# Loading the first two chunks of a gated recurrence as one pair, and re-planning the order of all engines, in a fused attention and gated MLP kernel

## The chip, the core and the metric

The kernel runs on one core of a Trainium2 chip. The core has five engines, each with its own queue of instructions that runs strictly in the order in which the program issued them: TensorE (PE, matrix products), VectorE (DVE), ScalarE (ACT), GpSimd (POOL) and SyncE (SP), which here only issues transfers. Sixteen DMA engines move data between the main memory and the on-chip memory. The metric is the device time of one execution in microseconds; the span of a profile is a little shorter, since it begins with the first instruction.

## What is computed

The first half is a gated recurrence over 768 steps for 4 batches and 8 heads with a state of 48 x 48; the second half is a gated MLP whose gate mixes the time steps with a matrix.

```python
# first half: q, k, v, alpha are (4, 8, 768, 48), float32
for t in range(S):
    state = alpha[:, :, t, :, None] * state + einsum('bhd,bhe->bhde', k[:, :, t], v[:, :, t])
    y[:, :, t] = einsum('bhd,bhde->bhe', q[:, :, t], state)

# second half: x is y as (4, 768, 384); d_ff = 1024
h = maximum(x @ w_in, 0)
u, v = h[..., :512], h[..., 512:]
v_n = (v - mean(v)) / sqrt(var(v) + 1e-6)
v_s = einsum('ts,bsd->btd', w_spatial, v_n) + b_spatial[None, :, None]
out = (u * v_s) @ w_out                      # (4, 768, 384), float32
```

## The kernel before

The 768 steps of a batch are cut into 6 chunks of 128, so there are 24 chunks, numbered through all four batches. A chunk turns the recurrence into matrix products: the logarithm of alpha (Ln on ACT), its running sum by a product with a triangle of ones (`cum`), two exponentials, the scaled keys and queries (`kt`, `qt`), their transposes, the scores, a causal mask, and the output `y`; beside it a state of 48 x 48 per head is carried from chunk to chunk (`upd`, `z`, `S`, `sb`).

There are two forms of this work. `first(i)` treats one chunk: each of its four loads brings 128 x 8 runs of 48 floats. `pair(j)` treats two neighbouring chunks at once: time steps 2p and 2p+1 lie side by side on partition p, so each load brings 128 x 8 runs of 96 floats for both chunks, and the running sum, scores and `y` are split into an even and an odd half (`par`) with two triangles (`le_pair`, `lt_pair`) and another mask (`mask2`).

```python
PAIRS = (1, 2)                     # chunks 2,3 and 4,5 go as pairs; all others one by one

def first(i):                      # one chunk
    def load(name, src):
        ...
        nc.sync.dma_start(out=t, in_=src[b, :, t0:t0 + C, :].rearrange("h s d -> s h d"))
    dma(("ac", i), LD, load("ac", alpha), ...)     # then kc, qc, vc
    ...

def pair(j):                       # chunks 2j and 2j+1
    def load(name, src):
        ...
        nc.sync.dma_start(
            out=t.rearrange("p h a d -> p h (a d)"),
            in_=src[b, :, t0:t0 + 2 * C, :].rearrange("h (p a) d -> p h (a d)", a=2))
    ...                            # ac, kc, qc, vc
    op(("lnp", j), "ACT", 0.73, ln, got(("ac", 2 * j), ("cz", 2), ("cz", 0)) + ...)
    for par in range(2):
        # cump, einvp, eexpp, ebc, ktp, qtp, vbp, transposes tr, evictions ev
        op(("ktp", j, par), {"POOL": 0.87, "DVE": 0.47}, ...)
        ...
```

The program's order is found before it is built. Every piece of work is an `Op` with a duration for each engine that may do it, and `schedule` places them one by one on the engine where they can start earliest; a table of small delays or advances (`PATIENCE`) bends the choice. What it decides is the order in each engine's queue, and which engine does an operation. Wherever the plan leaves TensorE idle in the first 40 us (`WARM`), it puts in products of a tile `junk` that nobody reads, which keep TensorE's clock up.

```python
def dma(key, us, emit, deps, prio, eng="SP", issue=0.99, lat=1.9):
    o = op(key + ("issue",), eng, issue, emit, deps, prio=prio)
    return op(key, "DMA", us, lambda _: None, [o], prio=prio, lat=lat)

o.wait = PATIENCE.get(key[0], 0.0)
```

The constants come first in the queues of DVE (memsets) and POOL (triangles and masks). Those of single chunks come ahead, those of pairs after them:

```python
def constants(_):
    nc.gpsimd.memset(ut_ones, 0.0)          # triangle of single chunks
    nc.vector.memset(junk, 0.5)
    nc.vector.memset(lap_bufs[0].bitcast(FP32), 0.0)
    ... # select on ut_ones, ident
    nc.vector.memset(mask4.bitcast(FP32), 0.0)
    nc.gpsimd.affine_select(out=mask4, ...) # mask of single chunks

def zeros(n):
    # n == 0: second set of la, kt, qt;  n == 1: sbd, ones_row, eps, lt_pair, mask2 to zero
    # n == 2: le_pair, lt_pair and the four quarters of mask2, by selects on POOL
    ...
```

The second half works in groups on one bank of the accumulation memory: `v` (x with the second half of w_in, then the mean and variance of each row, `bn`), `u` (first half of w_in), `s` (the mix over time, then the bias and the product with u), `o` (w_out). The output tiles are copied by ACT and stored; the last four go into the space that the raw weights have left, and the very last is copied by ACT and DVE, one half each. All of that is in the kernel before and stays.

Of the kernel before, what the change touches and what calls it, by code (L numbers as in the profile page):

```python
# [9 lines left out]
FP32 = mybir.dt.float32  # L10
BF16 = mybir.dt.bfloat16
AF = mybir.ActivationFunctionType
ALU = mybir.AluOpType
# [38 lines left out]
class Clock:  # L52
# [21 lines left out]

PATIENCE = {"ev": -0.3, "v": -0.1, "be": 0.2, "g": -0.3, "sb": -0.1, "bb": 0.5, "ln": 0.2, "z": -0.2, "we": -0.1, "S": 0.3, "cast": -0.1, "rs": 0.1, "trk": -0.1, "xs": -0.3}
ENGINES = {
    "kt": {"POOL": 0.87},
    "vb": {"POOL": 0.47},
    "S": {"POOL": 0.57},
    "sb": {"POOL": 0.79, "DVE": 0.36},  # L80
# [5 lines left out]
}  # L86
PAIRS = (1, 2)
ACT_STATS = ((2, 2), (1, 4), (1, 2))
PIECES = {
    "w_in": ((0, "vc", 0, 0.35), (0, "kc", 2, 0.15)),  # L90
    "w_sp": ((0, "vc", 4, 0.35), (0, "ac", 7, 0.05), (0, "ac", 7, 0.05)),
    "w_out": (0, "kc", 7, 0.15),
# [48 lines left out]
def kernel(  # L141
# [12 lines left out]
    nc = tc.nc  # L154
# [37 lines left out]
    fill = []  # L192
# [45 lines left out]
    def constants(_):  # L238

        nc.gpsimd.memset(ut_ones, 0.0)  # L240
        nc.vector.memset(junk, 0.5)  # L241
        nc.vector.memset(lap_bufs[0].bitcast(FP32), 0.0)
        nc.vector.memset(ones_col, 1.0)
        nc.gpsimd.affine_select(
            out=ut_ones, in_=ut_ones, compare_op=ALU.is_gt, fill=1.0,
            base=0, channel_multiplier=1, pattern=[[-1, 128]],
        )
        for t in (ktp_bufs[0], qtp_bufs[0]):
            nc.vector.memset(t.bitcast(FP32), 0.0)
        make_identity(nc, ident)  # L250
        nc.vector.memset(mask4.bitcast(FP32), 0.0)
        nc.gpsimd.affine_select(
            out=mask4, in_=mask4, compare_op=ALU.is_gt, fill=1.0,
            base=0, channel_multiplier=1, pattern=[[0, 4], [-1, 128]],
        )

    def zeros(n):

        def emit(_):
            if n == 0:  # L260
                for t in (lap_bufs[1], ktp_bufs[1], qtp_bufs[1]):
                    nc.vector.memset(t.bitcast(FP32), 0.0)
            if n == 1:
                for t in sbd_bufs:
                    nc.vector.memset(t.bitcast(FP32), 0.0)
                nc.vector.memset(ones_row, 1.0)
                nc.vector.memset(eps_tile, LN_EPS)
                nc.vector.memset(lt_pair.bitcast(FP32), 0.0)
                nc.vector.memset(mask2.bitcast(FP32), 0.0)
            if n == 2:  # L270
                nc.gpsimd.memset(le_pair, 0.0)
                for t, base in ((le_pair, 0), (lt_pair, 1)):
                    nc.gpsimd.affine_select(
                        out=t, in_=t, compare_op=ALU.is_gt, fill=1.0, base=base, channel_multiplier=1,
                        pattern=[[-1, 128]],
                    )
                    nc.gpsimd.memset(t[0:64, 64:128], 0.0)
                for par in range(2):
                    for ci in range(2):
                        rows = slice(64 * ci, 64 * ci + 64)  # L280
                        nc.gpsimd.affine_select(
                            out=mask2[rows, par], in_=mask2[rows, par], compare_op=ALU.is_gt, fill=1.0,
                            base=par, channel_multiplier=2, pattern=[[0, 4], [-1, 2], [-2, 64]],
                        )
        return emit
# [4 lines left out]
    def op(key, *args, **kw):  # L290

        users = kw.pop("use", ())
        o = Op(*args, **kw)
        for s in users:
            s.users.append(o)
        ops.append(o)
        made[key] = o
        o.wait = PATIENCE.get(key[0], 0.0)
        return o

    def got(*keys):
        return [made.get(x) for x in keys if x is not None]

# [85 lines left out]
    def pair(j):  # L389
# [30 lines left out]

        op(("lnp", j), "ACT", 0.73, ln, got(("ac", 2 * j), ("cz", 2), ("cz", 0)) + io_users("cum", jo, 0), prio=P + 1)
        sl_c = [Slot(rings["p2"]), Slot(rings["p2"])]
# [166 lines left out]
    def first(i):  # L589
# [15 lines left out]
        jo = j - NKP  # L605
        dma(("ac", i), LD, load("ac", alpha), io_users("ln", j), P)
        dma(("kc", i), LD, load("kc", k), io_users("kt", j), P + 0.1)
        dma(("qc", i), LD, load("qc", q), io_users("qt", j), P + 0.2)
        dma(("vc", i), LD, load("vc", v), io_users("vb", j), P + 0.3)

# [4 lines left out]

        op(("ln", i), "ACT", 0.41, ln, got(("ac", i), ("cz", 0) if j % NKP else None) + io_users("cum", jo, 0), prio=P + 1)

# [364 lines left out]
    op(("cz", 0), "DVE", 1.7, zeros(0), prio=-5.0)  # L982
    op(("cz", 1), "DVE", 1.3, zeros(1), prio=-4.0)
    op(("cz", 2), "POOL", 2.6, zeros(2), got(("cz", 1)), prio=-3.0)

# [38 lines left out]
    dma(("b_sp",), 0.1, lambda _: nc.gpsimd.dma_start(out=b_sp_sb, in_=moe_b_spatial[None, :]), [], 0.9, "POOL", 1.0)  # L1024
    late.append((made[("b_sp", "issue")], ("qc", 0)))
    for i in range(N):
# [56 lines left out]
```

## Time and profile before

The time is 159.15 us, the median of three runs (159.13 to 162.23). The profiled run has a span of 157.4 us with a granted clock of 1.0.

| What | Value |
|---|---|
| PE busy | 146.9 us, 93% of the span, 1719 matmuls |
| of it on `junk` | 15.1 us |
| DVE busy | 127.3 us, 81% |
| ACT busy | 108.4 us, 69% |
| POOL busy | 84.3 us, 54% |
| transfers | 28.6 MB, 97,173 packets, of which 92,032 under 512 B |
| first load issued, first Ln starts | 0.75 us, 3.77 us |
| last load issued | 108.85 us |
| last matmul ends | 153.7 us |

Read it as two questions. First, which engine is full in which stretch of the span, and how much of it is real work. Second, how early the first real work of each kind begins, since all later work of a full engine moves with it. A busy PE is not a PE at its peak: `junk` counts as busy.

### The profile page before, as it was taken

Reading aid. Unit: us, or ns where it says so; the run is one execution under the profiler, and the core shown is the slowest. Engines: PE = TensorE matmul, PEld = TensorE weight load, DVE = VectorE, ACT = ScalarE, POOL = GpSimd, SP = SyncE. Lnnn points to the kernel's source line nnn. Section 1 sums busy time; section 2 is a strip of 40 time slices with the busy share of each in tenths; the row PEclk is TensorE's granted clock in tenths of the full one; section 3 lists DMA queues with packets and bytes.
Section 4 is the critical chain, followed back from the end, with each engine's and each line's share of the span. In section 5 each row is a group of like instructions: output and inputs, shape, how many; then the busy total and the mean of one; then the engine's idle time right before and its main releaser. Section 6 shows DMA issues by size and latency. Waiting matters only on the chain.

```text
span 157.4 us, 4483 instructions
## 1 busy us (share of the span) xinstructions
PE 146.9 (93%) x1719; PEld 97.1 (62%) x1719; DVE 127.3 (81%) x271; ACT 108.4 (69%) x269; POOL 84.3 (54%) x141
## 2 busy tenths in 40 slices
PE   6849999998999998899999999999999999999990
PEld 5838577766667565456565657565675766556550
DVE  7617778879899999977899989899989989555820
ACT  3352786898897776589998465989996465891051
POOL 4684383645348754882236989654356956102420
PEclk9999999999999999999999999999999999999999
DMA  5999999989997999999897999998990000520034
GB/s 103 198 280 259 311 270 239 298 156 307 171 274 147 209 255 176 218 208 200 159 205 149 210 209 182 199 198 168 315 369 15 6 0 0 199 105 0 0 127 175
DMA packets 97173, 28.60 MB, mean 182 GB/s; under 512 B 92032, under 2 KB 95616, under 8 KB 97152
## 3 DMA queue, kind: packets, MB, share of 16 engines
q1 hardware_dynamic: 97120, 28.32, 77.6%
q8 instruction: 13, 0.21, 0.6%
q14 instruction: 8, 0.07, 0.1%
q0 software_dynamic: 32, 0.00, 0.0%
HBM read 23.60 MB, written 4.72 MB: 180 GB/s over the span
## 4 chain that ended last, share of the span: by engine, by line
PE 64%; DVE 22%; ACT 5%; issue 3%; POOL 3%; POOLq 0%; DVEq 0%
PE ps L774 38%; PE pt L671 4%; DVE ptm L712 4%; PE pt L701 3%; DVE vsb L914 2%; PE y L362 2%; DVE qt L654 2%; PE y L729 2%; DVE stats L836 2%; DVE sbd L209 2%; PE ps L199 2%; PE tp L687 2%; ACT x_sb L207 2%; DVE kqT L209 1%; PE y L723 1%
## 5 line engine op out<-in xcount | busy, mean ns | idle before, releaser
L927 POOL TENSOR_TENSOR gT<-vsb,uT 128x384 bf16<-128x384 f32 x28 | 25.5, 918 | 22.0 <-DVE vsb L914 21.6
L774 PE MATMUL ps<-w_spT,vn 128*128 128x384 bf16 x192 | 36.2, 326 | 0.3 <-DVE w_spT L209 0.3
L712 DVE TENSOR_TENSOR ptm<-pt,mask 128x512 bf16<-128x512 f32 x40 | 26.1, 682 | 2.0 <-PE pt L701 1.8
L644 POOL TENSOR_TENSOR kt<-kc,binv 128x384 bf16<-128x384 f32 x20 | 18.2, 914 | 13.3 <-ACT bc L639 9.0
L774 PEld LDWEIGHTS <-vn 128*128 128x128 bf16 x192 | 17.0, 97 | 10.8 <-issue 0.7
L333 POOL TENSOR_TENSOR state<-state,bc 128x192 f32<-128x192 f32 x20 | 10.3, 515 | 21.1 <-DVE state L328 14.0
L914 DVE TENSOR_TENSOR vsb<-ps,bsp_bc 128x384 f32<-128x384 f32 x31 | 16.6, 550 | 4.0 <-PE ps L774 3.5
L774 PE MATMUL ps<-w_in,xT 128*128 128x512 bf16 x72 | 19.4, 380 | 0.3
L207 ACT CAST x_sb<-y 128x384 bf16<-128x384 f32 x24 | 11.4, 477 | 10.4 <-PE y L729 8.9
L774 PE MATMUL ps<-xT,w_in 128*128 128x384 bf16 x96 | 18.4, 325 | 0.0
L774 PE MATMUL ps<-w_out_sb,gT 128*128 128x384 bf16 x96 | 18.1, 326 | 0.0
L209 DVE COPY kqT<-pt 128x1024 bf16<-128x1024 bf16 x17 | 11.5, 683 | 6.0 <-PE pt L671 5.9
L836 DVE BATCH_NORM_STATS2 stats<-v_sb 128x6 f32<-128x512 bf16 x18 | 12.3, 685 | 3.4 <-ACT v_sb L213 3.4
L213 ACT ACTIVATE v_sb<-ps 128x512 bf16<-128x512 f32 x18 | 10.8, 598 | 5.0 <-PE ps L774 4.6
L207 ACT COPY xT<-y 128x384 bf16<-128x384 bf16 x24 | 11.4, 480 | 3.5 <-PE y L362 3.2
L199 PEld LDWEIGHTS <-junk 128*128 128x128 bf16 x128 | 12.0, 109 | 2.3 <-DVE junk L241 1.1
L614 ACT ACTIVATE la<-ac 128x384 bf16<-128x384 f32 x20 | 10.4, 528 | 4.0 <-DMA ac<-in_alpha_dram 4.0
L209 POOL CAST vb<-vc 128x384 bf16<-128x384 f32 x20 | 10.1, 509 | 3.9 <-PE y L729 2.5
L774 PEld LDWEIGHTS <-gT 128*128 128x128 bf16 x96 | 8.8, 97 | 5.6
L866 DVE TENSOR_SCALAR vn<-v_sb,mvs,rstd 128x512 bf16<-128x512 bf16 x24 | 11.7, 521 | 0.2
L654 DVE TENSOR_TENSOR qt<-qc,cum 128x384 bf16<-128x384 f32 x20 | 10.8, 548 | 0.8 <-ACT cum L649 0.6
L774 PEld LDWEIGHTS <-w_in 128*128 128x128 bf16 x96 | 8.4, 97 | 4.6
(127 smaller groups left out, 299.2 us busy)
## 6 DMA issues: line engine op xcount, KB each, us to landing
ac<-in_alpha_dram SPq DMA_DIRECT2D x20, 192.0 KB, 4.1
kc<-in_k_dram SPq DMA_DIRECT2D x20, 192.0 KB, 4.1
qc<-in_q_dram SPq DMA_DIRECT2D x20, 192.0 KB, 4.1
vc<-in_v_dram SPq DMA_DIRECT2D x20, 192.0 KB, 4.1
raw_w<-in_moe_w_spatial_dram SPq DMA_DIRECT2D x3, 768.0 KB, 5.9
out_dram<-raw_w SPq DMA_DIRECT2D x12, 192.0 KB, 2.7
out_dram<-o_sb SPq DMA_DIRECT2D x9, 192.0 KB, 1.9
raw_w<-in_moe_w_in_dram SPq DMA_DIRECT2D x2, 768.0 KB, 6.5
```

The costliest lines, as they stand in the source:

```text
L199: nc.tensor.matmul(out=flat[:, 0:cols], lhsT=junk[:, 0:128], rhs=junk[:, 0:cols], start=True, stop=True)
L207: nc.scalar.copy(out=out, in_=in_)
L209: ENG[eng].tensor_copy(out=out, in_=in_)
L213: nc.scalar.activation(out=out, in_=in_, func=AF.Relu)
L644: ENG[eng].tensor_mul(out=kt[:, :, :, 0:D], in0=quad(st["kc"]), in1=st["binv"])
L654: nc.vector.tensor_mul(out=qt[:, :, :, 0:D], in0=quad(st["qc"]), in1=st["cv"])
L712: nc.vector.tensor_tensor(out=st["ptm"][:, s], in0=st[f"pt{s}"], in1=mask4, op=ALU.mult)
L774: return lambda ps: nc.tensor.matmul(out=out(ps), lhsT=lhsT(), rhs=rhs(), start=start, stop=stop)
L836: nc.vector.bn_stats(out=stats, in_=d["v_sb"][:, tt, :])
L866: nc.vector.tensor_scalar(out=d["vn"][:, t, :], in0=d["v_sb"][:, t, :], scalar1=d["mvs"][:, t, 0:1], scalar2=d["rstd"][:, t:t + 1], op0=AL ...
L914: nc.vector.tensor_tensor(out=hold["vs"], in0=ps[:, 0:TH], in1=bsp_bc[:, th, :], op=ALU.add)
L927: ENG[eng].tensor_tensor(out=bt[b]["gT"][:, dsl, cols], in0=hold["vs"], in1=bt[b]["uT"][:, dsl, cols], op=ALU.mult)
```

## The change

Chunks 0 and 1 are loaded and treated as a pair too, so that all six chunks of the first batch go as three pairs (`PAIRS = (0, 1, 2)`). It is for fewer and longer packets at the start and for two chunks in one pass. The constants of pairs now come ahead of those of single chunks, and the running sum of a pair no longer waits for the constants of single chunks.

The order is planned anew. The landing of a single chunk's load is planned at 2.9 us after its transfer time and no longer at 1.9 (`LATE`), while pairs and weights keep 1.9: hence uneven landings. A second table, `NUDGE`, delays or advances thirty named operations. `vb` may now go to ACT as well as POOL, the state's scaling `S` to DVE as well as POOL. One pair of `v` tiles whose statistics ACT computes is moved from batch 1 to batch 3, the last two pieces of the mixing matrix are loaded about one chunk earlier, and the load of the bias is issued after the first vc and no longer after the first qc.

The diff, with the cuts marked:

```diff
-PATIENCE = {"ev": -0.3, "v": -0.1, "be": 0.2, "g": -0.3, "sb": -0.1, "bb": 0.5, "ln": 0.2, "z": -0.2, "we": -0.1, "S": 0.3, ...}
+PATIENCE = {"ev": -0.3, "kt": -0.1, "v": -0.1, "sb": 0.3, "bb": 0.5, "ln": 0.2, "z": -0.2, "we": -0.1, "S": 0.2, ..., "xe": -0.2}
 ENGINES = {
-    "vb": {"POOL": 0.47},
-    "S": {"POOL": 0.57},
+    "vb": {"POOL": 0.47, "ACT": 0.42},
+    "S": {"POOL": 0.57, "DVE": 0.27},
 ...
-PAIRS = (1, 2)
-ACT_STATS = ((2, 2), (1, 4), (1, 2))
+NUDGE = {
+    ("o", 3, 0, "mm", 0): -0.15,
+    ("bn", 0, 1): -0.6,
+    ("kt", 6): 1,
+    ("ktp", 0, 0): -1.5,
+    ("v", 0, 4): -1.5,
+    ... # 25 more
+}
+PAIRS = (0, 1, 2)
+LATE = 2.9
+ACT_STATS = ((2, 2), (1, 4), (3, 4))
 PIECES = {
     "w_in": ((0, "vc", 0, 0.35), (0, "kc", 2, 0.15)),
-    "w_sp": ((0, "vc", 4, 0.35), (0, "ac", 7, 0.05), (0, "ac", 7, 0.05)),
+    "w_sp": ((0, "vc", 4, 0.35), (0, "qc", 6, 0.25), (0, "qc", 6, 0.25)),
 ...
     def constants(_):
-        nc.gpsimd.memset(ut_ones, 0.0)
         nc.vector.memset(junk, 0.5)
+        nc.gpsimd.memset(le_pair, 0.0)
+        nc.vector.memset(mask2[:, 0].bitcast(FP32), 0.0)
 ...     # selects for le_pair, lt_pair and mask2 move here from zeros(2);
 ...     # those for ut_ones and mask4 move to zeros(2)
-        o.wait = PATIENCE.get(key[0], 0.0)
+        o.wait = PATIENCE.get(key[0], 0.0) + NUDGE.get(key, 0.0)
 ...
-        op(("lnp", j), "ACT", 0.73, ln, got(("ac", 2 * j), ("cz", 2), ("cz", 0)) + ...)
+        op(("lnp", j), "ACT", 0.73, ln, got(("ac", 2 * j), ("cz", j - 1)) + ...)
 ...
-        dma(("ac", i), LD, load("ac", alpha), io_users("ln", j), P)
+        dma(("ac", i), LD, load("ac", alpha), io_users("ln", j), P, lat=LATE)
 ...     # the same for kc, qc, vc
-    late.append((made[("b_sp", "issue")], ("qc", 0)))
+    late.append((made[("b_sp", "issue")], ("vc", 0)))
```

The number of instructions in the queues changes as follows: four loads of 384 KB take the place of eight of 192 KB; PE has 117 products of `junk` in place of 128 and 58 products of other kinds more; DVE has 2 instructions more; ACT and POOL have as many as before, of other kinds.

## The prediction

> **What bounds the kernel now.** I read the busy shares and the slices first. The columns of the first five lines are busy time, share of the span and instructions; a digit below is the busy share of a slice of 3.9 us, in tenths.
>
> ```profile
> PE 146.9 (93%) x1719; PEld 97.1 (62%) x1719; DVE 127.3 (81%) x271; ACT 108.4 (69%) x269; POOL 84.3 (54%) x141
> ...
> PE   6849999998999998899999999999999999999990
> ...
> DVE  7617778879899999977899989899989989555820
> ACT  3352786898897776589998465989996465891051
> POOL 4684383645348754882236989654356956102420
> ...
> DMA  5999999989997999999897999998990000520034
> ```
>
> PE is at nine tenths from the fourth slice on, DVE nearly so from slice 8 to 33, the transfers from the second slice to the 31st. All three look like the bound, so I next asked for busy time by stretches (columns: stretch, length, then busy time and instructions of PE, PEld, DVE, ACT and POOL, granted clock, share of the DMA engines, GB/s).
>
> ```profile
> 8.00:12.00 4.00, 1.89 (x32) 1.42 (x32) 0.85 (x2) 2.17 (x5) 3.31 (x6) 1.00 1.07 276
> ...
> 36.00:40.00 4.00, 3.36 (x83) 2.79 (x81) 3.92 (x9) 2.96 (x8) 2.23 (x4) 1.00 1.07 293
> ...
> 116.00:128.00 12.00, 12.00 (x163) 8.27 (x160) 10.59 (x24) 7.72 (x19) 7.72 (x11) 1.00 0.19 67
> ```
>
> The same stretches for the line that issues `junk` alone give 15.11 us in all, of which 14.90 before 40 us and 0.21 after. So in the first 40 us PE is busy 35.3 us but does real work for only 20.4; after 40 us it is real work, 111.4 us in the 113.7 us up to the last matmul at 153.7. **The second part is a full PE with DVE just behind; only the first 40 us have room.** The transfers are no bound later: the last load is issued at 108.85 us, and 41 us of full PE follow its landing (some 4 us on). What does the start wait for? The timeline (start, duration, engine, line, operation):
>
> ```profile
> 0.75 0.43 SPq L601 DMA_DIRECT2D ac<-in_alpha_dram  x1
> ...
> 3.77 0.52 ACT L614 ACTIVATE la<-ac 128x384 bf16<-128x384 f32 x1 [1.74 <-DMA ac<-in_alpha_dram]
> ...
> 6.04 2.79 POOL L281 TENSOR_SCALAR_AFFINE_SELECT mask<-mask 64x512 bf16<-64x512 bf16 x4
> ...
> 9.53 0.91 POOL L644 TENSOR_TENSOR kt<-kc,binv 128x384 bf16<-128x384 f32 x1
> ...
> 17.38 0.81 PE L774 MATMUL ps<-w_in,xT 128*128 128x512 bf16 x3
> ...
> 21.41 0.81 PE L774 MATMUL ps<-w_in,xT 128*128 128x512 bf16 x3
> ```
>
> The first Ln is ready at 3.77 and its exponential `binv` at 5.44 (4.95 + 0.49), but the first `kt` starts at 9.53: POOL is still making the masks of pairs and issuing the bias's load. Four microseconds are lost there to constants that chunk 0 doesn't need. The last two lines are the `v` groups of chunks 0 and 1, four microseconds apart.
>
> **What the Trainium skill says.** "DMA: Bandwidth & Descriptors", section "Why small descriptors are slow (HBM only)", says that each packet has a fixed overhead, so short runs lose. The trace agrees: in 72 to 84 us, with single chunks alone, the engines move 190 GB/s at a share of 0.97; in 17 to 21 us, mostly pairs, 322 GB/s at 1.08. "TensorE: Matmul & The Clock Gate", section "What's actually happening", says that the array's clock is throttled until it has been active; the first 16 products of `junk` take 2.69 us here (168 ns each), 12 of them after 12.2 us take 1.15 (96 ns), so the filler is needed and its time is no saving by itself. "GPSIMD Engine Reference", section "Elementwise — side-by-side cycle accounting", puts an elementwise product of two tensors at 1.96 times DVE's time; here `kt` takes 912 ns on POOL and 552 on DVE, 1.65 times. This matters since the first `kt` half of the new pair goes to DVE.
>
> **The change, part by part.**
>
> *1. Transfers.* Eight loads of 196,608 B become four of 393,216 B with as many packets each (1024), so 4096 packets go. One single load is 196,608 / (190/0.97 GB/s) = 1.00 us of all 16 engines, one pair load 393,216 / (322/1.08) = 1.32 us. Saved: 4 x (2.00 - 1.32) = 2.7 us, all in the first ten microseconds of the stream. Every later load can land up to 2.7 us earlier; the order of bytes up to the second pair's vc is nearly the old one.
>
> *2. The first alpha.* It is twice as large: I add 0.3 us (1.32 - 1.00) to 3.77, so Ln starts at 4.1 and takes 0.84 for a pair, not 0.53.
>
> *3. The first pair's chain*, with durations of the second pair's rows: sums on PE 1.0 (two products with triangles of 0.33 and eight small ones of 0.04), to 5.95; `binv` 0.49, to 6.45. DVE's memsets add up to 5.2 us from 0.86, so it is free at 6.1 and does the first `kt` half to 7.0; POOL, with 5.3 us of selects, is free at about 6.8 and does the second (0.91) from 7.5 to 8.4. Queries: 8.8. Transposes and evictions (0.40 and 0.42 to 0.58): 9.9. vc lands at about 9 (2.9 us of latency as for the first load, four times 1.32, and the issue at 0.75) and its two casts on ACT share the time to 10.4. Scores to 10.9, four masks of 0.68 to 13.7, `y` of both chunks to 14.6, the cast, transpose and copy (0.48 + 0.34 + 0.48) to 15.9 and 16.3. So `v` of chunks 0 and 1 run at about 16.0 and 16.8 in place of 17.4 and 21.4: **1.4 and 4.6 us earlier.** The second half of w_in comes after five pair loads, as many bytes as before, and is cast by then.
>
> *4. The second pair.* Its `y` starts at 27.72 before. Its alpha comes fifth in the queue and its Ln can start at about 11 to 12, not at 17.20; its vc is 2.7 us earlier. DVE's queue up to its last mask holds about 21 us from 0.86 with the rows' means. I take `y` at 23 to 25: **3 to 5 us earlier.**
>
> *5. PE's own work.* By shape, a pair whose first chunk reads no state costs 1.1 (sums) + 0.67 (small) + 0.85 (scores) + 1.15 (`y`) + 0.35 (state) + 0.87 (`upd`) = 5.0 us; two single chunks 2 x (0.33 + 0.25 + 0.40 + 0.39 + 0.31) + 0.34 = 3.7. So 1.3 us more of real PE work, but at a time when PE has 15 us of filler; 11 fewer products of `junk` (about 1.1 us) take its place. Cost at the end: 0.
>
> *6. Moved work.* On DVE: eight casts of `sbd` fewer (-3.2), `kqT` +0.6, three `S` +1.05, two `uT` +1.1, one `gT` +0.6, one `kt` +0.55, weight casts -0.2: +0.5 us in 127, no relief. ACT gets five `vb` (+2.5) and gives up two `uT` (-1.0) and two weight casts: within 1 us. Nothing is taken off the engines that are full later.
>
> *Sum.* The front gains 3 to 5 us. Behind it the engines are full of unchanged work, and loads land early enough: chunk 6's alpha is issued at 23.27 and used at 33.17, chunk 8's at 35.73 and used at 47.04, so with 4.1 us to land 5 us or more are spare, and the loads come 2.7 us earlier themselves. So nearly all of the front's gain could reach the end. I take off about 1 us because the new order after 40 us can't be expected to leave PE less than the 2.3 us of idle that it has there now, and may leave more: expected -2.8 us, 156.4.
>
> **The rivals.**
> - *The old start isn't the bound.* If DVE decides in 22 to 60 us (it is busy 3.92 of 4 us in the line above for 36 to 40), an earlier `v` only fills queues behind it. For it: DVE's total grows by 0.5. Against it: DVE is idle for 3.15 us of 8 to 12 and itself waits for the start. It would make 158 to 159.5.
> - *The queue heads stop.* The plan keeps 1.9 us for a pair's landing, while pair loads take 6.1 us from issue to landing in the median and single ones 4.1. ACT's queue has the casts of vc ahead of the second pair's Ln, and PE has `y` ahead of the second pair's transposes. If vc lands 2 us later than I think, all of that waits, and the front gains 1 to 2 us only: 157.5 to 158.5.
> - *The new order is worse later.* Thirty nudges and other engines for `vb` and `S` re-arrange 110 us that are already 98% full on PE; 3 us of new idle would swallow the gain, 5 would turn it: 160 to 161.
> - *The stream of loads was the pace.* Then the time falls by the 2.7 us of transfers: 156.5, the same number by another way. What speaks against it is the 41 us after the last landing.
>
> **Range and chances.** The sum is 156.4. The low end takes the whole 5 us and a tidier middle; the high end the third rival in a mild form: 153.4 to 160.6. The 2% limits are at 156.0 and 162.3. My middle lies just above the first, so faster by over 2% gets 0.40, within 2% 0.47, slower 0.13.
>
> **What would show it.** Right: the first `kt` before 7.5 us, `v` of chunk 1 before 17.5, the second pair's `y` before 25.5, 93,000 packets, the last load issued 2 to 4 us earlier, and the last `junk` ahead of 37 us of real time. The step of the sum fails if these hold and the time doesn't fall: then PE's idle after 40 us has grown. The steps of the front fail if Ln of the first pair starts after 5 us, or if ACT's first cast of vc waits for its load for over a microsecond.

## The result, and the profile after

The changed kernel takes 157.48 us (median; 157.30 to 157.88) against 159.13 us for an undisturbed run of the kernel before: 1.6 us less. The ratio of all compared runs is 0.9899, with a 95% interval of 0.9867 to 0.9931. The forecast was 2.8 us less; the sign is right and the size is not. One sentence is needed to read the ratios: the kernel before runs at 159.1, 160.7 or 162.1 us with a mean TensorE clock of 1.00, 0.989 or 0.979, and ratios count the first two levels, so I also set each median beside 159.13.

The page of the changed kernel, the lines that answer to those of before (busy time, share, instructions; slices in tenths; the load queue's packets, MB and share of the 16 engines):

```profile
PE 145.3 (93%) x1766; PEld 95.7 (62%) x1766; DVE 127.6 (82%) x273; ACT 108.1 (69%) x269; POOL 83.2 (53%) x141
...
PE   7799799999999999897989998999999999999990
...
DVE  7777578598899899976999999889989999367830
...
q1 hardware_dynamic: 92960, 28.32, 77.9%
```

PE's third slice is 9 where it was 4, so the front is fuller. But slice 19 (70 to 74 us) has fallen to 7, and before no slice between the third and the last was below 8. The fifth (16 to 19 us) has fallen from 9 to 7 as well; more on it below. The busy time by stretches says it more exactly. Columns: stretch, length, busy time and instructions of PE, PEld, DVE, ACT and POOL, granted clock, share of the DMA engines, GB/s. Two stretches of the kernel before, then three of the changed one:

```profile
0.00:40.00 40.00, 35.30 (x535) 27.30 (x535) 29.55 (x68) 25.35 (x58) 22.79 (x49) 1.00 1.01 241
...
60.00:84.00 24.00, 22.63 (x247) 13.65 (x246) 21.18 (x46) 20.00 (x57) 11.51 (x19) 1.00 1.01 198
```

```profile
0.00:40.00 40.00, 36.52 (x597) 27.75 (x598) 30.08 (x71) 27.09 (x61) 22.82 (x49) 1.00 1.02 246
...
60.00:84.00 24.00, 21.61 (x252) 13.16 (x250) 21.17 (x45) 19.72 (x52) 12.68 (x22) 1.00 0.97 191
84.00:116.00 32.00, 31.32 (x388) 20.37 (x386) 29.93 (x62) 25.92 (x70) 19.50 (x32) 1.00 0.95 214
```

In 60 to 84 us PE is idle for 24.00 - 21.61 = 2.4 us (before: 24.00 - 22.63 = 1.4); the waits of that stretch name `qt` on DVE (0.7), `xT` and `uT` on ACT (0.8 and 0.7). With the line of `junk` taken out (13.21 us, all before 40), the end of the last matmul is a sum that can be compared ("real work" is PE's busy time less that of `junk`):

| PE, in us | before | after | difference |
|---|---|---|---|
| `junk` | 15.1 | 13.2 | -1.9 |
| real work up to 40 us | 20.4 | 23.3 | +2.9 |
| real work after 40 us | 111.4 | 108.8 | -2.6 |
| idle up to 40 us | 4.7 | 3.5 | -1.2 |
| idle after 40 us | 2.1 | 3.1 | +1.0 |
| last matmul ends | 153.7 | 151.9 | -1.8 |

**The front hands over 2.6 us of work early, and 1.0 us of that is lost to new idle later.** Now the milestones of the front, and what stands ahead of the second pair's `y` (timeline: start, duration, engine, line, operation, idle before it and its releaser):

```profile
4.57 0.84 ACT L452 ACTIVATE la<-ac 128x768 bf16<-128x768 f32 x1 [2.55 <-DMA ac<-in_alpha_dram]
...
6.79 0.66 DVE L499 TENSOR_TENSOR kt<-kc,binvp 128x384 bf16<-128x384 f32 x1 [0.82 <-ACT binvp L479]
...
15.15 0.79 PE L606 MATMUL y<-vbp,ptm 64*128 64x48 bf16 x28
...
16.97 0.27 PE L606 MATMUL y<-vbp,ptm 64*128 64x48 bf16 x4 [1.02 <-issue]
...
18.48 1.47 PE L808 MATMUL ps<-w_in,xT 128*128 128x512 bf16 x6
...
19.34 1.25 ACT L246 ACTIVATE v_sb<-ps 128x512 bf16<-128x512 f32 x2 [0.39 <-PE ps L808]
...
21.44 0.66 DVE L870 BATCH_NORM_STATS2 stats<-v_sb 128x6 f32<-128x512 bf16 x1
...
22.35 0.30 ACT L892 ACTIVATE rstd<-mvs,eps_tile 128x2 f32<-128x2 f32 x1 [0.42 <-DVE mvs L871]
...
22.79 0.83 ACT L452 ACTIVATE la<-ac 128x768 bf16<-128x768 f32 x1
...
23.95 0.33 PE L463 MATMUL ps<-la,le_pair 128*128 128x384 bf16 x1
...
24.65 0.42 PE L579 MATMUL pt<-kqT 48*64 48x128 bf16 x16
...
26.99 0.57 PE L606 MATMUL y<-vbp,ptm 64*128 64x48 bf16 x16
```

Ln starts at 4.57 and the first `kt` at 6.79, not at 9.53. `v` of chunks 0 and 1 is one group at 18.48 to 19.95: for chunk 1 that is 2 us earlier, for chunk 0 1 us later. Read from there as a chain: `v` is copied by ACT, its statistics go to DVE, `rstd` to ACT, and only behind `rstd` in ACT's queue comes Ln of the *third* pair; PE's queue has the third pair's sums (23.95) ahead of the second half of the second pair's scores (24.65), and these gate the masks and `y` at 26.99. Before, that `y` came at 27.72. So the second pair gained 0.7 us. The third pair's two `y` come at 35.74 and 36.97 where they came at 38.30 and 39.08: the gain appears there. The kernel before, for the second and the third pair:

```profile
27.72 0.57 PE L572 MATMUL y<-vbp,ptm 64*128 64x48 bf16 x16
...
38.30 0.57 PE L572 MATMUL y<-vbp,ptm 64*128 64x48 bf16 x16
```

The fifth slice is the first pair's `y`, which stops for 1.02 us (16.97). The profile names nothing that PE waits for there. The page counts 14 transfers of 16 KB on the queue of kind `instruction` (q8); in the packed trace the first of them inside the span runs from 14.39 to 15.62 us, and PE goes on 1.35 us after its end. Of the kernels below, 1, 4, 10, 12, 13, 14, 16 and 17 have the same stop (0.8 to 1.35 us), each after 222 or 223 products on PE and 1.3 to 1.6 us after the end of that transfer, in kernel 4 three microseconds later than in the others. So it is most likely a wait of PE for its own instructions; no run tests that.

### The profile page after: what moved, and what is told of

Its sections match the earlier page's. It is cut to its first block, busy times and chain, and to the rows that moved or that the text cites. A ratio compares the mean times of both kernels' runs of the same rounds, so it can differ in the third digit from the quotient of the medians.

```text
span 155.6 us, 4579 instructions
## 1 busy us (share of the span) xinstructions
PE 145.3 (93%) x1766; PEld 95.7 (62%) x1766; DVE 127.6 (82%) x273; ACT 108.1 (69%) x269; POOL 83.2 (53%) x141
## 2 busy tenths in 40 slices
DMA packets 93014, 28.62 MB, mean 184 GB/s; under 512 B 87872, under 2 KB 91456, under 8 KB 92992
## 4 chain that ended last, share of the span: by engine, by line
PE 62%; DVE 11%; ACT 6%; issue 2%; POOL 1%; DVEq 0%
PE ps L808 41%; PE pt L705 4%; PE pt L735 3%; PE y L396 2%; DVE vsb L948 2%; DVE vn L900 2%; DVE ptm L746 2%; PE y L763 2%; PE tp L721 2%; PE y L757 1%; PE y L606 1%; PE cum L654 1%; DVE kqT L242 1%; PE ps L818 1%; DVE qt L688 1%
## 5 line engine op out<-in xcount | busy, mean ns | idle before, releaser
L961 POOL TENSOR_TENSOR gT<-vsb,uT 128x384 bf16<-128x384 f32 x27 | 24.6, 920 | 19.1 <-DVE vsb L948 18.8
L746 DVE TENSOR_TENSOR ptm<-pt,mask 128x512 bf16<-128x512 f32 x36 | 23.5, 682 | 1.3 <-PE pt L735 1.0
L678 POOL TENSOR_TENSOR kt<-kc,binv 128x384 bf16<-128x384 f32 x18 | 16.4, 914 | 12.3 <-ACT bc L673 7.9
L808 PE MATMUL ps<-w_in,xT 128*128 128x512 bf16 x72 | 18.7, 380 | 0.9 <-ACT xT L240 0.8
L367 POOL TENSOR_TENSOR state<-state,bc 128x192 f32<-128x192 f32 x17 | 8.7, 510 | 19.4 <-DVE state L362 8.5
L242 DVE COPY kqT<-pt 128x1024 bf16<-128x1024 bf16 x16 | 10.8, 681 | 1.4 <-PE pt L705 1.2
L232 PEld LDWEIGHTS <-junk 128*128 128x128 bf16 x117 | 10.6, 106 | 2.2 <-DVE junk L273 1.1
L242 POOL CAST sbd<-state 64x192 bf16<-64x192 f32 x30 | 10.4, 348 | 2.0 <-DVE state L367 0.8
L240 ACT COPY o_sb<-ps 128x384 f32<-128x384 f32 x9 | 4.3, 483 | 10.0 <-PE ps L808 9.8
L808 PEld LDWEIGHTS <-xT 128*128 128x128 bf16 x72 | 6.4, 98 | 7.0 <-ACT xT L240 2.0
```

The costliest lines, as they stand in the source:

```text
L232: nc.tensor.matmul(out=flat[:, 0:cols], lhsT=junk[:, 0:128], rhs=junk[:, 0:cols], start=True, stop=True)
L240: nc.scalar.copy(out=out, in_=in_)
L242: ENG[eng].tensor_copy(out=out, in_=in_)
L367: ENG[eng].tensor_tensor(out=st["state"], in0=st["state"], in1=st["bc"][:, :, None].to_broadcast([128, HP, D]), op=ALU.mult)
L678: ENG[eng].tensor_mul(out=kt[:, :, :, 0:D], in0=quad(st["kc"]), in1=st["binv"])
L746: nc.vector.tensor_tensor(out=st["ptm"][:, s], in0=st[f"pt{s}"], in1=mask4, op=ALU.mult)
```

## The experiments

All kernels and their times; "by 159.13" is the median divided by 159.13 us.

| kernel | us | ratio, 95% interval | by 159.13 |
|---|---|---|---|
| after | 157.48 | 0.9899 (0.9867 to 0.9931) | 0.990 |
| 1 pair alone, old tables | 160.32 | 1.0070 (1.0031 to 1.0108) | 1.007 |
| 2 new tables without the pair | 201.23 | 1.2622 (1.2569 to 1.2676) | 1.265 |
| 3 after without nudges | 158.44 | 0.9956 (0.9938 to 0.9974) | 0.996 |
| 4 after, late start | 161.18 | 1.0112 (1.0065 to 1.0160) | 1.013 |
| 5 as 2, without nudges | 162.36 | 1.0050 (1.0011 to 1.0089) | 1.020 |
| 6 before, masks of pairs later | 159.18 | 0.9991 (0.9958 to 1.0024) | 1.000 |
| 7 after, `kt` of the second pair ahead | 157.62 | 0.9900 (0.9854 to 0.9945) | 0.991 |
| 8 after, eleven operations ahead | 160.25 | 1.0037 (1.0008 to 1.0067) | 1.007 |
| 9 loads alone | 92.77 | no comparison | |
| 10 as 3, even landings | 157.10 | 0.9859 (0.9808 to 0.9910) | 0.987 |
| 11 as 4, with filler | 157.95 | 0.9902 (0.9861 to 0.9942) | 0.993 |
| 12 as 1, late landings | 160.38 | 0.9953 (0.9872 to 1.0034) | 1.008 |
| 13 as 10, old patience and engines | 153.85 | 0.9605 (0.9542 to 0.9668) | 0.967 |
| 14 as 10, old loads and statistics | 158.04 | 0.9875 (0.9800 to 0.9951) | 0.993 |
| 15 as 10, without the pair | 163.70 | 1.0187 (1.0094 to 1.0280) | 1.029 |
| 16 as 13, old statistics | 153.84 | 0.9621 (0.9546 to 0.9697) | 0.967 |
| 17 as 13, old loads of the matrix | 159.25 | 0.9977 (0.9947 to 1.0007) | 1.001 |
| 18 as 13, without the pair | 163.50 | 1.0230 (1.0162 to 1.0299) | 1.027 |

### 1. The pair alone

```diff
 # the kernel before
-PAIRS = (1, 2)
+PAIRS = (0, 1, 2)    # with the new order of the constants and Ln's new dependencies
```

> Pair and constants alone, with the old planning tables. Theory A (the time is decided by how much real work is done in the first 40 us, and the pair with its constants is what does more of it): 156.5 to 158.5 us, v of chunk 1 before 20 us, at least 1 us less filler and idle before 40 us. Theory B (the new plan is what helps, the pair is worth nothing): 158.8 to 160.5. Theory C (the pace of the loads): 158.2, that is only the saved transfer time of about 1 us.

Measured 160.32 us, slower than before. `v` of the first chunks is at 18.0 to 20, the second pair's `y` at 27.49, the third's at 39.26 and 43.59. The front does more (23.1 us of real work by 40 us for 20.4) and still nothing is gained: the third pair's second `y` comes 4.3 us behind its first, where 0.8 lay between them before. PE's idle after 40 us is recorded as 4.2 us for 2.1, but 18 of the 72 products of the `v` groups are missing from this trace. Three of them take 0.82 us and two 0.59, so one is 0.22 us; filled in where a gap is, the idle is about 2.7 us (an estimate). The pair is no gain with these tables; kernel 16 shows how little has to change.

### 2. The new tables without the pair

```diff
 # the changed kernel
-PAIRS = (0, 1, 2)
+PAIRS = (1, 2)       # with the old constants; nudges kept
```

> The new planning tables, other engine choices and moved pieces, with chunks 0 and 1 one by one and the old constants. Theory A: 158.5 to 160.5 us, no gain, v of chunk 1 still at 21 us. Theory B: 157 to 158. Theory C: 159.1, no packets saved.

201.23 us, with PE's clock down to 0.50 in stretches (60 to 65 and 120 to 130 us). Nudges name single operations of one plan; in another they do harm. This says nothing of the tables; kernel 5 repeats it without them.

### 3. The changed kernel without nudges

```diff
 # the changed kernel
-NUDGE = { ... 30 entries ... }
+NUDGE = {}
```

> The changed kernel without its thirty nudges. Theory A: the front is nearly the same, 157.3 to 158.5 us, with more idle of PE after 40 us than 3.2. Theory B: 159 or more. Theory C: 157.5, as the changed kernel.

158.44 us: nudges are worth 0.96 us. Real work by 40 us is 23.3 as with them. Where behind that they act the trace doesn't say: it records 4.4 us of idle after 40 us for 3.1, but 19 products of `v` are missing from it, and with them filled in as in kernel 1 the idle is about 3.0 (an estimate).

### 4. A later start

```diff
 # the changed kernel, Ln of the first pair
-nc.scalar.activation(out=lap[...], in_=st["ac"]..., func=AF.Ln)
+for _ in range(3 if j == 0 else 1):
+    nc.scalar.activation(out=lap[...], in_=st["ac"]..., func=AF.Ln)
```

> The changed kernel in the same order, with the first Ln done three times, 1.7 us later start of all that follows. Theory A (the front decides, nothing behind it has slack): 1.2 to 1.8 us slower than the changed kernel, 158.7 to 159.3. Rival of the prediction, DVE or the filler behind the front takes up the shift: under 0.6 us slower, 157.4 to 158.1. Theory C: no change, 157.5.

161.18 us: 3.7 us lost by a shift of 1.7. That is more than the start alone can cost, so something else moved; kernel 11 shows what.

### 5. The new tables without the pair and without nudges

```diff
 # kernel 2
-NUDGE = { ... }
+NUDGE = {}
```

> New planning tables with no nudges, chunks 0 and 1 one by one, constants as before: beside the kernel without nudges (158.4) it differs by the pair alone, beside the kernel before by the tables alone. Theory A (the pair helps once the plan is made with later landings): 159.0 to 160.5 us. Theory B (the tables help by themselves, the pair costs about 1 us as it did with the old tables): 157.0 to 158.0. If it is far above 165, a plan for single chunks with these tables is bad in itself and the nudges were not the cause of the 201 us.

162.36 us in the median; the lowest runs lie at 159.7 to 160.1, with a mean clock of 0.986 to 0.988, and by the ratio it is 159.9. Kernel 3, which has the pair, takes 158.44. Under the new tables the pair is worth 1.5 us by these lower runs, 3.9 by the medians, under the old ones -1.2: pair and order can't be told apart as parts of a sum.

### 6. The kernel before, with the masks of pairs out of the way

```diff
 # the kernel before, moves in the finished order
+for key in (("trk", 0), ("ev", 0), ("upd", 0), ("sc", 0)): move(key, ahead_of=("cum", 1))
+for key in (("m", 0, 0), ("m", 0, 1), ("S", 0), ("kt", 1)): move(key, ahead_of=...)   # casts of w_in
+move(("cz", 2), behind=("vb", 1))      # the constants of pairs on POOL
```

> The kernel before, in its own order except that the masks of pairs on POOL come after the first two kt and vb, and the first chunk's transposes, state product, scores and masks come before the second chunk's sums. The first kt then starts at 5.5 to 6.5 us and not at 9.5. If the old start was the bound (point 1 of the prediction): v of chunk 0 at 15 to 16, of chunk 1 at 18.5 to 20, the whole 1 to 2 us faster than before, 157.1 to 158.2. If other waits (loads, DVE) bound the front behind it: within 0.5 us of before, 158.7 to 159.5.

159.18 us, no change. The first `kt` is at 5.23 (9.53 before) and chunk 0's `v` at 15.67, but chunk 1's is at 21.69 and the second pair's `y` at 28.96, later than before. (In this profile PE's clock is 0.57 in 20 to 24 us, so the two later times are in part the clock's.) The 4 us of waiting for POOL, which my reading of the profile made the first loss to be won, are worth nothing in this order.

### 7. The second pair's `kt` transposes ahead of the first pair's second `y`

```diff
 # the changed kernel, moves in the finished order
+for par in (0, 1): move(("tr", "k", 1, par), ahead_of=("y", 1))
```

> The changed kernel with one move on PE: the two transposes of kt of the second pair stand between y of chunks 0 and 1 and not behind both. If PE's queue heads are what holds the front (second rival of the prediction): DVE's copies of kt start about 1.4 us earlier (16.4 and not 17.8), y of the second pair 0.5 to 1.5 us earlier than 27.0, the time 0.3 to 1.3 us lower, 156.2 to 157.2. If the loads or DVE hold it: within 0.3 us of 157.5.

157.62 us, no change: DVE copies the transposes at 16.17 and not 17.77, and the second pair's `y` is at 27.07. That queue head isn't the limit.

### 8. Eleven operations moved ahead in the first 25 us

```diff
 # the changed kernel, moves in the finished order
+move(("sc", 0, 1), ahead_of=("cump", 1, 1))   # half-scores ahead of the next pair's sums
+move(("sc", 1, 1), ahead_of=("cump", 2, 0))
+move(("sc", 1, 0), ahead_of=("bb", 0))
+move(("lnp", 2), ahead_of=("be", 0))          # third pair's Ln
+for par in (0, 1): ...                        # transposes of the second pair ahead of y and v
```

> The changed kernel with eleven operations of the first 25 us moved ahead of work that stands in their way: scores ahead of the next pair's sums, transposes of the second pair's kt and qt and their copies ahead of y and v, the third pair's Ln ahead of the bias copy. If the order in the queues holds the front: y of the second pair at 23.5 to 25.5, the time 155.5 to 156.8. If it is the landing of the second w_in piece and of the second pair's vc (both near 19 to 20 us): y of the second pair not before 26, the time 157 to 158.

160.25 us, worse. Scores ahead of the sums put PE behind the masks (waits of 0.87 and 0.62 us), the third pair's sums went to 26.9, and the second pair's `y` to 30.27. About 1 us of that is the clock, which is 0.57 in 24 to 28 us: 14 products of `junk` take 2.39 us there, 1.31 in the changed kernel. Runs with a mean clock of 1.00 take 159.2 us and more as well, so my order was worse than the plan's by over 1.5 us.

### 9. Loads by themselves

This kernel leaves out the whole computation: it loads 48 single chunks and then 24 pairs, as many bytes of each, and stores zeros.

```diff
+for n in range(48): nc.sync.dma_start(out=t, in_=src[b, :, c*C : c*C+C, :]...)      # 192 KB each
+for n in range(24): nc.sync.dma_start(out=t, in_=src[b, :, c*C : c*C+2*C, :]...)    # 384 KB each
+for n in range(24): nc.sync.dma_start(out=out[...], in_=zero)
```

> Loads alone, no compute: 48 loads of single chunks, then 24 of pairs with the same bytes in all, then the stores of a tile of zeros. If a pair load costs 1.32 us of the engines as the prediction worked out, the first 9.4 MB take about 48 us and the second 9.4 MB about 32. If the saving of 0.9 us in four loads that the two profiles show is right, a pair costs about 1.78 us and the second half takes about 43 us.

Its busy times by stretches (only DVE and POOL are listed), the first of single loads, the second of pairs; the last number is GB/s:

```profile
4.00:44.00 40.00, 0.00 (x0) 0.00 (x0) 1.00 1.09 214
46.00:74.00 28.00, 0.00 (x0) 0.00 (x0) 1.00 1.12 307
```

A single load takes 196,608 B / 214 GB/s = 0.92 us of the engines, a pair's 393,216 / 307 = 1.28: each pair saves 2 x 0.92 - 1.28 = 0.56 us, four of them 2.2. That agrees with the Trainium skill, "DMA: Bandwidth & Descriptors", section "Why small descriptors are slow (HBM only)", as the forecast read it. In the kernel the queue's share is 0.779 x 155.6 = 121.2 us after and 0.776 x 157.4 = 122.1 before: 0.9 us saved. The last load is issued at 107.24 for 108.85.

### 10. Even landings

```diff
 # kernel 3
-LATE = 2.9
+LATE = 1.9
```

> The changed kernel without nudges and with all landings planned at 1.9 us. If the later landing of single chunks is what makes the plan fit the chip: 159.5 to 161 us, beside 158.4 with it. If it is worth nothing: 158.0 to 158.8.

157.10 us: better than with uneven landings (158.44), and without any nudge as good as the changed kernel. The late landing isn't what makes the order fit.

### 11. The later start, with filler

```diff
 # kernel 4, ahead of the first sums on PE
+ 16 products of junk
```

> The kernel with the first Ln done three times (161.2 us), with 16 products of junk more ahead of the first sums, so that PE doesn't stand idle for the 2.4 us of the shift. If that kernel lost twice its shift because PE's clock fell: granted clock 1.0 in all slices, 158.8 to 159.6 us, that is the shift of 1.7 us and no more. If the order alone makes the loss: 160.8 to 161.5.

157.95 us: 3.2 us come back by adding work that nobody reads. First kernel 4, then this one, the same three stretches (the eighth column is the clock):

```profile
4.00:8.00 4.00, 1.57 (x19) 1.08 (x17) 1.91 (x8) 2.57 (x4) 2.78 (x6) 0.95 1.28 262
8.00:12.00 4.00, 4.00 (x42) 3.31 (x41) 2.42 (x5) 2.42 (x7) 1.52 (x2) 0.63 1.15 322
...
20.00:24.00 4.00, 3.77 (x29) 1.94 (x30) 2.08 (x5) 1.94 (x4) 1.50 (x4) 0.65 1.04 243
```

```profile
4.00:8.00 4.00, 3.23 (x36) 2.60 (x33) 1.92 (x8) 2.63 (x4) 2.80 (x6) 1.00 1.28 261
8.00:12.00 4.00, 4.00 (x68) 3.36 (x67) 2.77 (x6) 3.21 (x10) 1.53 (x2) 1.00 1.15 321
...
20.00:24.00 4.00, 4.00 (x66) 2.79 (x64) 3.16 (x9) 3.50 (x8) 1.19 (x4) 1.00 0.97 248
```

Without filler PE is idle for 2.43 us ahead of the first sums and then works at 0.63 of its clock. With it, the start is still 1.7 us late, the second pair's `y` comes at 27.51, 0.5 later, and the time is 0.5 us above the changed kernel's. The wait of kernel 4, then the chain of kernel 11:

```profile
7.14 0.32 PE L464 MATMUL ps<-la,le_pair 128*128 128x384 bf16 x1 [2.43 <-ACT la L453]
```

```profile
16.64 1.12 PE L624 MATMUL y<-vbp,ptm 64*128 64x48 bf16 x32
...
19.01 1.47 PE L826 MATMUL ps<-w_in,xT 128*128 128x512 bf16 x6
...
25.18 0.42 PE L597 MATMUL pt<-kqT 48*64 48x128 bf16 x16
...
27.51 0.57 PE L624 MATMUL y<-vbp,ptm 64*128 64x48 bf16 x16
```

The first pair's `y` starts 1.5 us late (16.64 for 15.15) but runs through without the stop of 1.02 us. The 0.5 us that are left stand in everything behind it: `v` (19.01 for 18.48), the half of the scores (25.18 for 24.65), `y` (27.51 for 26.99) and the time. **So a start 1.7 us later costs 0.5 us, since the stop in the first pair's `y` takes up the rest; behind it the shift arrives in full, and no slack shows.** An earlier start wasn't tried.

### 12. The pair alone with late landings

```diff
 # kernel 1
+LATE = 2.9     # on the loads of single chunks
```

> Pair and constants with the old tables (160.2 us) and the later landing of single chunks alone added. If the later landing is what makes the pair pay: 157.5 to 158.8 us. If the other tables do (weights' places, engines for vb and S, small delays): 159.7 to 160.7.

160.38 us in the median, 158.08 at best, all at a clock of 0.965 to 0.988: unclear.

### 13 and 14. Which tables

```diff
 # kernel 13: kernel 10 with PATIENCE, "vb" and "S" of the kernel before
-PATIENCE = {"ev": -0.3, "kt": -0.1, ..., "sb": 0.3, ..., "xe": -0.2}
+PATIENCE = {"ev": -0.3, ..., "be": 0.2, "g": -0.3, "sb": -0.1, ...}
-    "vb": {"POOL": 0.47, "ACT": 0.42}, "S": {"POOL": 0.57, "DVE": 0.27},
+    "vb": {"POOL": 0.47}, "S": {"POOL": 0.57},
 # kernel 14: kernel 10 with the loads and statistics of the kernel before
-ACT_STATS = ((2, 2), (1, 4), (3, 4));  "w_sp": (..., (0, "qc", 6, 0.25), (0, "qc", 6, 0.25));  b_sp behind ("vc", 0)
+ACT_STATS = ((2, 2), (1, 4), (1, 2));  "w_sp": (..., (0, "ac", 7, 0.05), (0, "ac", 7, 0.05));  b_sp behind ("qc", 0)
```

> The version without nudges and with even landings (157.1 us), with the old table of patience and the old engines for vb and S; the old pieces of the mixing matrix's loads, the old choice of rows whose statistics ACT computes and the old place of the bias's load are not restored. Theory: the gain between the second and third pair comes from the choice of engines (vb on ACT, S on DVE) and the patience, so this goes back to about 159.5 to 160.5 us and the third pair's y to 38 or later. Rival: it comes from the moved loads and statistics; then this stays at 157 to 157.8 and the third pair's y at 36 to 37.

> The version without nudges and with even landings (157.1 us), with the old pieces of the mixing matrix's loads, the old choice of rows whose statistics ACT computes and the old place of the bias's load; patience and engines stay new. Theory that patience and engines make the gain: this stays at 157 to 158 us with the third pair's y at 36 to 37.5. Rival that the moved loads and statistics make it: 159.5 to 160.5, with more idle of PE after 40 us. If both this and the kernel with the old patience and engines lose about as much, the gain is a fit of all tables to one order and no single part has it.

Kernel 13 runs in 153.85 us (153.71 to 154.46), against both expectations: the old patience and engines don't lose the gain, they more than double it. It beats the kernel before and the changed one. Kernel 14 takes 158.04. The stretches of kernel 13:

```profile
0.00:40.00 40.00, 36.94 (x608) 28.23 (x609) 32.22 (x74) 27.57 (x62) 23.88 (x49) 1.00 1.01 245
...
60.00:84.00 24.00, 23.72 (x287) 15.34 (x286) 21.57 (x46) 20.89 (x56) 15.06 (x26) 1.00 1.00 197
84.00:116.00 32.00, 31.77 (x369) 20.49 (x368) 29.13 (x64) 25.99 (x69) 19.49 (x30) 1.00 0.99 229
```

Its front is that of the changed kernel: 13.8 us of `junk`, 23.2 of real work by 40 us (after: 13.2 and 23.3), the second pair's `y` at 26.83, the third's at 36.63 and 37.41. What differs is behind it: the last matmul ends at 149.0 us with 108.3 of real work after 40 us, so 0.7 us of idle in place of 3.1.

### 15. Kernel 10 without the pair

```diff
 # kernel 5
-LATE = 2.9
+LATE = 1.9
```

> The new tables without nudges and with even landings, but chunks 0 and 1 one by one, with the old constants; it differs from the 157.1 us version in the pair alone. Theory: the pair is worth about 1.5 us when the tables fit it, as with the later landings (159.9 against 158.4), so this takes 158.3 to 159.5 us. Rival: the new tables alone bring the gain and the later landing was what cost single chunks their time; then this is within 0.6 us of 157.1. The third rival, that the pair is worth more than 2.5 us here, would show 159.6 or more.

163.70 us; every run has a clock below 1 (0.954 to 0.989). The pair is worth 6.6 us here, in part by the clock.

### 16, 17 and 18. What makes kernel 13 good

```diff
 # kernel 16: kernel 13 with the old statistics
-ACT_STATS = ((2, 2), (1, 4), (3, 4))
+ACT_STATS = ((2, 2), (1, 4), (1, 2))
 # kernel 17: kernel 13 with the old loads of the mixing matrix
-"w_sp": (..., (0, "qc", 6, 0.25), (0, "qc", 6, 0.25))
+"w_sp": (..., (0, "ac", 7, 0.05), (0, "ac", 7, 0.05))
 # kernel 18: kernel before with the loads, statistics and bias of kernel 13; chunks 0 and 1 one by one
```

> The 153.85 us version (pair, old patience and engines, moved loads and statistics, even landings, no nudges) with the old choice of the rows whose statistics ACT computes, (1, 2) in place of (3, 4). Theory: the moved statistics keep DVE from being late in batch 1, so PE's idle after 40 us grows from 0.7 to 2 us or more and the time to 155.5 us or more. Rival: the earlier loads of the mixing matrix are what matters; then this stays at 153.5 to 154.5.

> The 153.85 us version with the last two pieces of the mixing matrix loaded in their old places. Theory that the loads matter: 156 to 160 us and the third pair's y at 38 us or later. Rival that the statistics matter: 153.5 to 154.5. If this and the kernel with the old statistics both lose 2 us or more, the gain is a fit of the order and belongs to no part.

> The kernel before with the moved loads, the moved statistics and the bias's load after the first vc, chunks 0 and 1 one by one; it differs from the 153.85 us version in the pair and its constants alone. Theory: the pair brings its real work earlier only where the order behind it lets PE take it, and is worth 2 to 4 us here: 156 to 158 us for this kernel. Rival: the moves alone are the gain and the pair is worth nothing: 153.5 to 154.5. Third: the moves fit only with the pair: 159 us or more.

The statistics don't matter (153.84). The place of two loads does: 159.25, 5.4 us more, with the same pair, patience and engines. The second piece is issued at 31.19 and not 29.32, the third at 41.18 and not 42.81, and PE's order after 37 us is another. PE in kernel 13, then in kernel 17 (the last line of each is the first mix over time, `s`):

```profile
36.63 0.57 PE L575 MATMUL y<-vbp,ptm 64*128 64x48 bf16 x16
...
37.41 0.57 PE L575 MATMUL y<-vbp,ptm 64*128 64x48 bf16 x16
...
45.31 0.65 PE L777 MATMUL ps<-w_spT,vn 128*128 128x384 bf16 x3
```

```profile
37.07 0.56 PE L575 MATMUL y<-vbp,ptm 64*128 64x48 bf16 x16
...
39.66 0.59 PE L777 MATMUL ps<-w_in,xT 128*128 128x512 bf16 x2 [0.18 <-issue]
...
40.39 0.83 PE L787 MATMUL ps<-ident,w_row 128*128 128x128 bf16 x12
...
41.65 0.57 PE L575 MATMUL y<-vbp,ptm 64*128 64x48 bf16 x16
...
49.05 0.65 PE L777 MATMUL ps<-w_spT,vn 128*128 128x384 bf16 x3
```

The third pair's second `y` and the first `s` both come about 4 us later (41.65 for 37.41, 49.05 for 45.31). The masks that this `y` reads are done by 36.8 in both kernels; in kernel 17 PE's queue has the first chunk's `v`, twelve transposes of the mixing matrix and 13 products of `junk` ahead of it. The same lag of 4.2 to 4.6 us behind the first `y` stands in all three kernels with the pair, even landings and the old places of these loads (1, 14 and 17), and 0.8 us in all three with the new places (10, 13 and 16). The lag isn't the whole loss, though: between 10 and 14 the time differs by 0.9 us only. The last matmul ends 4.2 us later (153.2 for 149.0): 1.4 us of that are `junk` (15.2 for 13.8), and the idle after 40 us is about 2.4 us for 0.7 (recorded 3.5, with 17 missing products filled in as in kernel 1).

Kernel 16 is also kernel 1 with these two loads and the load of the bias moved, and with no other difference: 153.84 us for 160.32. **So the pair with the old tables and these moved loads gains 5.3 us over the kernel before, more than three times what the changed kernel gains.** By kernels 13 and 17 the two loads of the matrix make most of that difference.

And kernel 18, the same moves without the pair, takes 163.50. Its front:

```profile
8.00:12.00 4.00, 2.11 (x18) 1.90 (x18) 0.69 (x1) 0.14 (x1) 3.44 (x6) 0.63 0.99 264
12.00:16.00 4.00, 3.49 (x38) 3.06 (x36) 3.10 (x6) 2.07 (x5) 1.85 (x3) 0.51 1.03 241
```

PE has nothing to do in half of 8 to 12 us, and its clock falls. By 40 us it has done 18.5 us of real work as recorded; kernel 13 has done 23.2.

## Why the prediction was right in its mechanism and wrong in its size

The step that failed is the front's share of the sum, "the front gains 3 to 5 us", and in it step 4. I worked with 3.8 (2.8 expected, plus the 1 us taken off). By the table of PE's time, 2.6 us less real work is left at 40 us, and 0.2 us of `junk` after 40 us is gone: 2.8. Then 1.0 is lost to idle, leaving 1.8 us of span. The missing microsecond is the front's. The stop in the first pair's `y` (1.02 us) is as long, and by kernel 11 what stands behind it moves the end one for one; that it is the missing microsecond is my estimate, since no run takes it out alone.

- *Step 1, transfers, mis-sized.* 2.7 us forecast, 0.9 measured in the kernel. Kernel 9 gives 2.2 for the four loads alone, so 0.5 is the durations that I took from a mixed stream; why 1.3 us more are lost in the kernel's own mix isn't settled.
- *Step 2, alpha.* Ln at 4.57, forecast 4.1, inside the 5 us that would have failed it.
- *Step 3, the first pair's chain, right to 12 us and then late.* `kt` at 6.79 and the first scores at 10.27 (forecast done by 10.9) hold. The second half of the scores stands on PE behind the second pair's sums and runs at 12.99; `y` starts at 15.15 for about 13.7 and has the stop of 1.02 us in it; `v` of chunk 1 is at about 19.2 for 16.8. The gain of 4.6 us there is 2.2, and the 1.4 of chunk 0 has become a loss of 1.1.
- *Step 4, the second pair, wrong.* `y` at 27.0, forecast 23 to 25. I followed the pair's own loads and DVE's queue. The trace shows another path: `v`, statistics, `rstd`, the third pair's Ln and sums, and the half of the scores behind them. Kernels 7 and 11 bear it out: a transposed `kt` of the pair 1.6 us earlier leaves that `y` where it was, and the half microsecond by which `v` is late in kernel 11 goes through every member of this path to it. That breaking this path would win the time is not shown: kernel 8 tried and made it worse.
- *Step 5, PE's own work.* 1.3 us forecast; real work is 132.1 us for 131.8, so 0.3. It costs nothing at the end, as said.
- *Step 6, moved work.* The totals of DVE and ACT moved by +0.3 and -0.3 us; right.
- *The loss after 40 us.* "About 1 us" forecast, 1.0 measured. The forecast was a margin that named no wait, so that the figure fits is luck. And kernel 13, with the same front, has 0.7 us of idle and 153.85 us: 1.4 us less idle than the kernel before. So the loss belongs to this order and not to the pair.

Of the signs that I named, `kt` before 7.5, 93,014 packets and ACT's wait for vc (0.72 us) hold; `v` of chunk 1, the second pair's `y`, the last load (1.6 us earlier, not 2 to 4) and the last `junk` (38.56, not before 37) don't.

Of the rivals, the queue heads come nearest: half-scores behind sums that wait for another engine, and 157.5 to 158.5 forecast for it; the landing of vc that I named as its cause wasn't it. The old start as no bound is half right: a first `kt` 4.3 us earlier wins nothing in kernel 6, but what the stop leaves of a later start reaches the end in full in kernel 11. The worse order is right for 1 us. The stream of loads as the pace is out, since 0.9 us of transfers were saved and 2.8 of PE's time.

**What the pair is worth has no single number.** With the rest the same it is 1.2 us slower under the old tables (kernel 1), 1.5 faster (3 against 5), 6.6 faster (10 against 15) and 9.7 faster (13 against 18). In all four it brings real work into the first 40 us, 2.7 to 6.1 us of it as recorded (missing products are worth up to 0.5): 23.1 for 20.4, 23.3 for 19.0, 24.2 for 18.1, 23.2 for 18.5. Whether that reaches the end is decided by the order behind it, and in part by the clock: in kernels 5, 15 and 18 PE's clock falls in the gap that single chunks leave. If a mean clock near 0.979 costs there what it costs the kernel before (162.1 for 159.1), about 3 us of the 6.6 and of the 9.7 are the clock's; that is an estimate.

Open are the cause of the stop in the first pair's `y`, for which only the instruction transfer speaks (kernels 3 and 11, which reach that place later, have none), the 1.3 us of transfers, and by which rule of the plan two loads' places put 4 us of other work ahead of one `y`; the last is shown as a fact of the order, not explained.

## What to carry to other kernels

A part that fills the front of a kernel pays only as far as the order behind it lets the full engine take the work: count real work done by a fixed time and the idle after it as two terms, and measure both, after counting whether the trace has all products: by my estimate 18 missing ones made 1.5 us of the recorded idle of kernel 1. In a planned kernel, one change and its tables are one thing: nine planned orders of the same pair ran between 153.8 and 160.4 us, so a part is judged with the order re-planned for it, and a table of fixes for single operations is compared with a run that has none (kernel 10 equals the changed kernel without any). When the queues are in order, follow what stands ahead of an operation in its queue, not only what it reads.

## What the hardware showed that I had not expected

PE's clock falls after gaps shorter than I thought. In kernel 4's profile an idle of 2.43 us, in a stretch of 4 us with 1.57 busy, was followed by a stretch at 0.63 of the clock, and a stretch with 2.65 us busy (16 to 20 us) by one at 0.65. With 16 products of filler in the first gap every stretch up to 40 us has 1.00, and the time is 3.2 us lower, 2% of it. Not all of that is the clock: the first pair's `y` starts 1.2 us earlier with the filler (16.64 for 17.81), and its stop of 1.35 us is gone. Nor do the mean clocks settle the share, since two of kernel 4's five runs record 1.00 and take 161.2 us all the same. The Trainium skill, "TensorE: Matmul & The Clock Gate", section "HAM oscillation — how this bites in real kernels", gives gaps over about 3.4 us as the ones to avoid; here a shorter one was enough. Little work in one stretch doesn't decide it alone: the kernel before has 1.89 us of it in 8 to 12 us and keeps 1.00 there.
